# More added matrix products behind steps 2 and 3, a free bank for others, a third buffer for q and k

## The chip, the cores and the metric

The kernel runs on one core of one Trainium2 chip. The metric is the device time of one execution in microseconds (us). A core has engines that work side by side, each through its own queue of instructions in a fixed order: TensorE (PE in the profile, with its weight loads as PEld), VectorE (DVE), ScalarE (ACT), GpSimd (POOL) and SyncE (SP), which here only issues DMA transfers. An instruction waits in its queue until what it needs is done, and what is queued behind it waits too.

## What is computed

Windowed attention with linear biases over 8 batches, 8 heads, 576 positions and a head size of 64, and behind it a layer that takes the largest of three matrix products:

```python
scores = scale * np.matmul(q, k.transpose(0, 1, 3, 2))
mask = (rel >= 0) & (rel < window)                  # window = 128
scores = np.where(mask, scores + bias[None], -1000000000.0)
scores = scores - np.max(scores, axis=-1, keepdims=True)
attn = np.exp(scores)
attn = attn / (np.sum(attn, axis=-1, keepdims=True) + 1e-09)
attn_out = np.matmul(attn, v)
...
x = attn_out.transpose(0, 2, 1, 3).reshape(B * S, H * D)     # 4608 x 512
h = np.maximum(np.maximum(x @ w1, x @ w2), x @ w3)           # 4608 x 768
return h @ w_out                                             # 4608 x 512
```

## The kernel before

**Attention.** Work goes by *tasks*: one task is one pair of heads of one batch, so there are 4 tasks in a batch and 32 in all. A task has four blocks of 128 queries and a rest of 64; the rests of two tasks are done together. That gives 18 *steps* in a batch (`steps`, L406). The first batch runs: steps 0 to 4 belong to the first pair (step 4 holds the rests of the first and second pair), steps 5 to 8 to the second, steps 9 to 13 to the third, and so on.

For each two steps `products` (L413) puts score products of 64x64 tiles of PE into PSUM: into the tile `ps_s`, or, for steps 2, 6, 10 and 14 with the step behind each, into two banks of `ps_m`. For each step `score` (L438) has DVE move masked parts (L447, L450) and add the bias with a running minimum (L461); `exps` (L469) has ACT take exponentials; `sums_of` (L477) has ACT and DVE make the reciprocals; `normalise` (L482) multiplies, some on POOL (L487), some on ACT (L492); `turn` (L494) has PE transpose two steps into the bank `pt` (four instructions, L500), ACT copy them out (L504, L509, L512), and POOL cut out the window (L520, L524); `mix` (L529) multiplies with v (L545).

**The layer behind.** The weights come as packed integers. `fetch` (L150) loads a group (12 in all), `exponents` (L163) and `convert` (L173) turn it into floats on DVE, `part` (L210) splits it into a high and a low part and stores it; two buffers take the groups in turn, so a fetch waits until the group two before it is stored. `plain` (L769) runs the products of the first two batches (L791, L767 for three that begin early), `unit` (L812) those of the later ones in a form with fewer products (L846).

**Order.** All of it is written as events with due times, counted in steps (`at`, L872), sorted and called in that order (L950). The scheduler of the framework then lines up each engine's queue from its own estimate of what is ready, earlier calls first; `keep_in_program_order` puts an instruction behind the one called before it on its engine. From due time 46 on (`fix`, L935) this holds for nearly all of PE. A tile pool with n buffers hands a buffer on when the last reader of the tile in it is done.

**What the change touches.** `spin` (L372) issues n matrix products of zeros (128x512, bfloat16; L375) into the bank `pt`, the one in which `turn` puts its transposes. Their result is not read: the text calls them added products. Four run at the very start (L940), four are due at each of 3.45, 5.45, 7.45, ... 17.45 (L932), and ten stand behind the first plain products (L775). Each is kept behind what was called before it on PE. The group due at 3.45 comes behind the score products of steps 2 and 3, the one at 5.45 behind the transposes of steps 0 and 1 and the score products of steps 4 and 5.

`load` (L389) gets q and k of one task into a buffer of `qk_p` (two buffers), issued by SP (L394); `load_v` (L396) gets v. The start (L940 to L949) issues on SP the first pair, the first weight group, the second pair, v of the first pair, and the second weight group. q and k of the third pair are due at 0.6 (the second step of the first pair, L880) and take the buffer of the first pair, so they wait for the score products of step 4; v of the second pair is due at 2.6 and stands behind them in SP's queue.

The tiles `xs` (pool `xs_p`, seven buffers of the same size as a tile of `qk_p`) hold the attention's results of a batch, high and low part, for the layer behind. The first are written at due time 14.3 (L904).

Of the kernel before, what the change touches and what calls it, by code (L numbers as in the profile page):

```python
# [8 lines left out]
F32 = mybir.dt.float32  # L9
# [10 lines left out]
LOAD_I = 1  # L20
# [5 lines left out]
AT = 0, 3, 1, 2, 4, 6, 5  # L26
PLAIN_AT = (0, 6), (4, 5)
RING = 2
SPIN, FIRST_SPIN = 4, 4


FEW = 6
# [5 lines left out]
def attention_maxout_kernel(  # L38
# [12 lines left out]
    P = 128  # L51
    B, NP, _, _, S = qk.shape
# [5 lines left out]
    NB = S // P  # L58
# [3 lines left out]
    qk_p = ctx.enter_context(tc.tile_pool(name="qk_p", bufs=2))  # L62
# [4 lines left out]
    xs_p = ctx.enter_context(tc.tile_pool(name="xs_p", bufs=7))  # L67
# [5 lines left out]
    ps_m = ctx.enter_context(tc.tile_pool(name="ps_m", bufs=1, space=PSUM))  # L73
    ps_s = ctx.enter_context(tc.tile_pool(name="ps_s", bufs=1, space=PSUM))
    ps_t = ctx.enter_context(tc.tile_pool(name="ps_t", bufs=1, space=PSUM))
# [74 lines left out]
    def fetch(g):  # L150
        r = raws[g] = raw_tile()
        nc.sync.dma_start(r[:, SMALL:].bitcast(U8)[:, :16 * DM - 3], w_all[g].bitcast(U8)[:, 3:])
# [216 lines left out]
    idle = hs_p.tile([P, P + 512], mybir.dt.bfloat16, name="hs")  # L369
    nc.vector.memset(idle, 0.0)  # L370

    def spin(n):  # L372
        spun = ps_t.tile([P, 512], F32, name="pt")
        for _ in range(n):
            tc.keep_in_program_order(nc.tensor.matmul(  # L375
                spun, lhsT=idle[:, :P], rhs=idle[:, P:], start=True, stop=True, skip_group_check=True,
            ))
# [8 lines left out]
    tasks = [(b, hp) for b in range(B) for hp in range(NP)]  # L386
    qkt, vt = {}, {}


    def load(t):  # L390
        b, hp = tasks[t]
        qkt[t] = qk_p.tile([P, 2, S], F32, name="qk")
        for cs in (slice(0, 2 * P), slice(2 * P, S)) if t == 0 else (slice(0, S),):
            nc.sync.dma_start(qkt[t][:, :, cs], qk[b, hp, :, :, cs])  # L394

    def load_v(t):  # L396
        b, hp = tasks[t]
        vt[t] = v_p.tile([P, NB + 1, P], F32, name="v")
        nc.sync.dma_start(vt[t], v[b, hp])
# [10 lines left out]
    n_steps = len(steps) // B  # L410
# [199 lines left out]
    xs, hs, hq = {}, {}, {}  # L610
# [158 lines left out]
    def plain(b, v):  # L769
# [4 lines left out]
        if b == 0 and v == 1:  # L774
            spin(10)  # L775
# [96 lines left out]
    def at(when, what, *args):  # L872
        events.append((when, len(events), what, args))
# [2 lines left out]
    where = {x: s for s, x in enumerate(steps)}  # L876
    for s, (t, i) in enumerate(steps):
        c = s + shift[tasks[t][0]]
        if i == LOAD_I and t + 2 < len(tasks):
            at(c - 0.4, load, t + 2)  # L880
        if i == NB - 1 and t + 1 < len(tasks):
            at(c - 0.4, load_v, t + 1)
        if i == 0 and 0 < t < NP:
            at(c - 1, slopes, t)
            if t % 2 == 0:
                at(c - 1, slopes_t, t // 2)
        at(c + 0.04, score, s)
        at(c + 0.3, exps, s)
        if s % 2 == 0:
            at(c + 0.002, products, s)  # L890
            at(c + DRAIN[0].get(n_steps - s, LAG_T) + 0.003, turn, s)
        else:
            at(c + (0.6 if s == n_steps - 1 else 1.1), sums_of, s)
            at(c + (0.8 if s == n_steps - 1 else 1.5), normalise, s)
# [34 lines left out]
    at(2.06, weights, 1)  # L929
    for s in range(5, n_steps + 2):  # L930
        at(s + 0.2, weights, 1.4 if s > 5 else 0.6)
    for s in range(3, n_steps, 2):  # L932
        at(s + 0.45, spin, SPIN)

    def fix():  # L935
        nonlocal fixed
# [1 line left out]

    at(2 * n_steps + LAG_X + shift[2], fix)
    spin(FIRST_SPIN)  # L940
    load(0)
    nc.scalar.dma_start(dist[:, 2], c_ident)
    fetch(0)
    slopes(0)
    slopes_t(0)
    load(1)
    load_v(0)
    nc.scalar.copy(out=plus, in_=dist[:, 2])
    fetch(1)  # L949
    for _, _, what, args in sorted(events, key=lambda e: e[:2]):  # L950
# [39 lines left out]
```

## Time and profile before

| | us |
|---|---|
| median of 3 runs | 750.51 |
| lowest and highest of them | 749.09 and 750.65 |
| the profiled execution | 752.57 |
| its span, first to last instruction | 750.9 |

The profile is of one execution. Its page gives busy time by engine; its views give stretches of time with the busy time of each engine and the clock that was granted to PE (1.00 is 2.4 GHz, 0.50 is 1.2 GHz), the instructions in order of time, the waits, the DMA issues with the time until they landed, and the chain of waits that ended last. A row of the timeline merges neighbouring instructions of one kind: "x4" is four of them, and the time is that from the start of the first to the end of the last.

### The profile page before, as it was taken

How to read it: one execution, taken by the hardware profiler on the slowest of the kernel's cores; microseconds unless marked ns; L12 is line 12 of the kernel's file. 1: busy time of each engine (PE TensorE's matmuls, PEld its weight loads, DVE VectorE, ACT ScalarE, POOL GpSimd, SP SyncE). 2: the span in 40 equal slices, each digit the busy share in tenths (PEclk: the TensorE clock that was granted, in tenths of full speed). 3: DMA queues.
4: the chain of work that ended last, by engine and by line, in shares of the span. 5: the costliest groups of instructions: out<-in, count | busy, mean ns of one | idle time of the engine just before them, and what ended most of it. 6: DMA issues, size and time to landing. Idle time of an engine off the chain costs nothing.

```text
span 750.9 us, 19281 instructions
## 1 busy us (share of the span) xinstructions
PE 733.9 (98%) x7209; PEld 674.6 (90%) x7214; DVE 515.2 (69%) x1614; ACT 487.2 (65%) x1603; POOL 236.4 (31%) x451
## 2 busy tenths in 40 slices
PE   7999989999999999999999999999999999999998
PEld 3459988999999999999999999999999999999998
DVE  4888887536659477784778567794777747683673
ACT  5786976766667767676677757776666767552342
POOL 4661224645556123212222123222222122343100
PEclk8999999999999999999999999999999999999999
DMA  7877999759998489855988378864988468899611
GB/s 252 274 282 298 330 340 331 253 187 340 361 349 275 134 279 303 273 181 192 322 294 276 116 266 304 291 213 146 330 289 273 163 228 272 252 291 355 230 61 64
DMA packets 57085, 192.81 MB, mean 257 GB/s; under 512 B 5792, under 2 KB 24480, under 8 KB 50464
## 3 DMA queue, kind: packets, MB, share of 16 engines
q0 software_dynamic: 20304, 108.54, 43.9%
q1 hardware_dynamic: 36400, 82.85, 31.2%
q8 instruction: 57, 0.93, 0.5%
q14 instruction: 36, 0.29, 0.1%
q10 hardware_dynamic: 288, 0.20, 0.1%
HBM read 156.95 MB, written 34.60 MB: 255 GB/s over the span
## 4 chain that ended last, share of the span: by engine, by line
PE 77%; DVE 11%; ACT 7%; DMA 2%; issue 1%; POOL 1%; SPq 0%; DVEq 0%; ACTq 0%; POOLq 0%
PE ps_m L846 46%; PE ps_m L791 16%; PE ps_s L431 5%; PE pt L500 4%; PE ps_x L567 4%; DVE hs L615 2%; DVE hq L733 2%; ACT p L473 2%; DVE t L732 2%; DMA qk<-in_qk 1%; PE ps_x L545 1%; DMA hs<-in_w_all 1%; ACT p L492 1%; DVE t L618 1%; DVE xs L615 1%
## 5 line engine op out<-in xcount | busy, mean ns | idle before, releaser
L846 PE MATMUL ps_m<-xs,ring 128*128 128x288 f32 x2160 | 302.7, 297 | 0.6
L846 PEld LDWEIGHTS ps_m<-xs,ring 128*128 128x128 f32 x2160 | 290.1, 188 | 3.7 <-ACT t L863 3.4
L520 POOL TENSOR_SCALAR_AFFINE_SELECT pp<-pr 128x256 f32<-128x256 f32 x112 | 53.9, 482 | 277.2 <-ACT pr L504 154.0
L473 ACT ACTIVATE p<-s,st 128x128 f32<-128x128 f32 x288 | 114.7, 400 | 20.8 <-DVE st L461 17.2
L863 ACT COPY t<-ps_m 128x288 f32<-128x288 f32 x196 | 76.7, 394 | 71.2 <-PE ps_m L846 69.5
L791 PE MATMUL ps_m<-xs,ring 128*128 128x288 f32 x846 | 118.1, 297 | 2.8 <-DVE hq L808 2.2
L791 PEld LDWEIGHTS ps_m<-xs,ring 128*128 128x128 f32 x846 | 113.3, 188 | 4.1 <-DVE hq L808 2.4
L367 POOL DMA_DIRECT2D ring<-keep x103 | 55.5, 539 | 165.5 <-PE ps_m L846 157.3
L846 PE MATMUL ps_m<-hs,ow 128*128 128x288 f32 x756 | 105.8, 297 | 0.4
L846 PEld LDWEIGHTS ps_m<-hs,ow 128*128 128x128 f32 x756 | 100.9, 188 | 2.6 <-ACT t L863 1.2
L492 ACT ACTIVATE p<-p,st 128x128 f32<-128x128 f32 x252 | 84.6, 393 | 24.1 <-DVE st L480 24.1
L732 DVE TENSOR_TENSOR t<-ps_m,t 128x288 f32<-128x288 f32 x108 | 48.8, 453 | 42.8 <-PE ps_m L846 32.5
L461 DVE CUSTOM_DVE_ANT_0 s<-ps_s,bias 128x128 f32<-128x128 f32 x240 | 60.6, 285 | 9.0 <-POOL bias_t L112 3.4
L431 PE MATMUL ps_s<-qk 64*64 64x192 f32 (+1 forms) x1088 | 62.0, 319 | 3.4 <-DMA qk<-in_qk 2.4
L614 ACT CAST hs<-hq 128x288 fp32r<-128x288 f32 x96 | 40.2, 432 | 30.8 <-DVE hq L733 18.1
L473 ACT ACTIVATION_READ_ACCUMULATOR p<-s,st 128x1 f32 x288 | 55.3, 192 | 0.0
L567 PE MATMUL ps_x<-pp,v 64*64 64x64 f32 (+3 forms) x1456 | 53.4, 274 | 0.1
L567 PEld LDWEIGHTS ps_x<-pp,v 64*64 64x64 f32 x1456 | 41.7, 133 | 10.5 <-issue 8.6
L500 PE MATMUL pt<-plus,p 128*128 128x128 f32 x288 | 48.5, 289 | 2.0 <-POOL p L487 1.3
L524 POOL TENSOR_SCALAR_AFFINE_SELECT pp<-pr 128x256 f32<-128x256 f32 (+1 forms) x112 | 50.0, 447 | 1.1
L733 DVE TENSOR_TENSOR hq<-t,hq 128x288 f32<-128x288 f32 x108 | 48.8, 457 | 2.1
L601 DVE TENSOR_TENSOR xk<-ps_x,xk 128x256 f32<-128x256 f32 (+3 forms) x56 | 25.4, 454 | 36.0 <-ACT xk L600 36.0
(94 smaller groups left out, 942.0 us busy)
## 6 DMA issues: line engine op xcount, KB each, us to landing
ring<-keep POOLq DMA_DIRECT2D x51, 1024.0 KB, 7.4
ring<-keep POOLq DMA_DIRECT2D x61, 768.0 KB, 6.1
qk<-in_qk SPq DMA_DIRECT2D x31, 576.0 KB, 5.3
hs<-in_w_all SPq DMA_DIRECT2D x12, 1023.6 KB, 7.2
v<-in_v SPq DMA_DIRECT2D x32, 320.0 KB, 6.5
outT<-t SPq DMA_DIRECT2D x64, 144.0 KB, 1.8
keep<-ring SPq DMA_DIRECT2D x9, 768.0 KB, 6.5
plain<-hs SPq DMA_DIRECT2D x12, 512.0 KB, 4.0
```

The lines of the kernel that those rows point to most:

```text
L367: nc.gpsimd.dma_start(wts[n, a], keep[n % 9][a])
L431: pe(nc.tensor.matmul(ps[j][d:d + D, o:o + k1 - k0], lhsT=qkt[u][j * D:(j + 1) * D, 0, q0:q0 + D], rhs=qkt[u][j * D:(j + 1) * D, 1, k0:k1] ...
L461: first(nc.vector.tensor_tensor_reduce(out=x, in0=ps[j][:, P:2 * P], in1=below, scale=-0.125, scalar=3.0e38, op0=ALU.add, op1=ALU.min, acc ...
L473: nc.scalar.activation(p[:, j], x, AF.Exp, bias=st[:, 0, a, j:j + 1], scale=-1.0, accum_out=st[:, 1, a, j:j + 1])
L492: nc.scalar.activation(p[:, j], p[:, j], AF.Copy, scale=st[:, 2, a, j:j + 1])
L500: pe(nc.tensor.transpose(out=pt[:, a, j], in_=p[:, j], identity=ident))
L567: pe(nc.tensor.matmul(x[j * D:(j + 1) * D, r, o:o + rhs.shape[1]], lhsT=vv[k, i, j * D:(j + 1) * D], rhs=rhs[k], start=start, stop=True, s ...
L732: nc.vector.tensor_tensor(out=s, in0=ps, in1=e, op=ALU.add)
L733: nc.vector.tensor_tensor(out=h, in0=s, in1=h, op=ALU.max)
L791: pe(nc.tensor.matmul(ps, lhsT=lt, rhs=rt, start=n == 0 and not (b == 0 and v < EARLY), stop=n == len(pairs) - 1, skip_group_check=True,))
L846: pe(nc.tensor.matmul(part_of[n, {2: 0, 5: 0, 6: 0, 3: 1}.get(kk, kk)], lhsT=lt, rhs=rt, start=first, stop=i == len(pairs) - 1, skip_group ...
L863: nc.scalar.copy(out=e, in_=ps)
```

## The change

1. The group of added products due at 3.45 has 13 instead of 4 (`WAIT_SPIN`) and writes the bank `ps_m2`, which at that time nothing else uses. The group due at 5.45 is dropped. The groups due at 7.45, 9.45, 11.45, 13.45 and 15.45 keep their four and write `ps_m2` too; the one at 17.45 stays as it was.
2. q and k of the third pair (task 2) go into a buffer of `xs_p`. They are issued at the start, behind v of the first pair, and v of the second pair behind them, both ahead of the second weight group. Their events at 0.6 and 2.6 fall away. The fourth pair then takes the first pair's buffer of `qk_p`, the fifth the second's; from the sixth pair on each waits for the same pair as before.

```diff
-SPIN, FIRST_SPIN = 4, 4
+SPIN, FIRST_SPIN, WAIT_SPIN = 4, 4, 13
...
-    def spin(n):
-        spun = ps_t.tile([P, 512], F32, name="pt")
+    def spin(n, spare=False):
+        spun = (ps_m if spare else ps_t).tile([P, 512], F32, name="ps_m2" if spare else "pt")
...
-        qkt[t] = qk_p.tile([P, 2, S], F32, name="qk")
+        qkt[t] = (xs_p if t == 2 else qk_p).tile([P, 2, S], F32, name="xs" if t == 2 else "qk")
...
-        if i == LOAD_I and t + 2 < len(tasks):
+        if i == LOAD_I and 2 < t + 2 < len(tasks):
             at(c - 0.4, load, t + 2)
-        if i == NB - 1 and t + 1 < len(tasks):
+        if i == NB - 1 and 1 < t + 1 < len(tasks):
             at(c - 0.4, load_v, t + 1)
...
-    for s in range(3, n_steps, 2):
-        at(s + 0.45, spin, SPIN)
+    at(3.45, spin, WAIT_SPIN, True)
+    for s in range(7, n_steps, 2):
+        at(s + 0.45, spin, SPIN, s < n_steps - 2)
...
     load_v(0)
+    load(2)
+    load_v(1)
     nc.scalar.copy(out=plus, in_=dist[:, 2])
     fetch(1)
```

## Rows read from the trace of the kernel before

**Rows 1.** The page: busy us (share of the span), instructions of each engine.

```profile
PE 733.9 (98%) x7209; PEld 674.6 (90%) x7214; DVE 515.2 (69%) x1614; ACT 487.2 (65%) x1603; POOL 236.4 (31%) x451
```

**Rows 2.** Stretches: length, busy of PE, PEld, DVE, ACT, POOL; clock, DMA, GB/s.

```profile
8.85:11.26 2.41, 0.00 (x1) 0.00 (x1) 1.47 (x7) 0.79 (x4) 1.56 (x4) 0.86 1.05 427
11.26:17.30 6.04, 5.82 (x34) 2.71 (x35) 3.10 (x16) 3.93 (x18) 1.50 (x4) 0.50 0.66 249
...
25.00:54.20 29.20, 27.68 (x229) 14.88 (x227) 25.00 (x84) 24.37 (x89) 18.06 (x27) 1.00 0.86 310
...
57.52:123.00 65.48, 61.58 (x645) 56.78 (x645) 55.42 (x160) 51.33 (x145) 17.35 (x31) 1.00 0.89 326
123.00:750.90 627.90, 623.44 (x6204) 593.62 (x6203) 418.22 (x1307) 394.87 (x1308) 186.28 (x362) 1.00 0.74 248
```

**Rows 3.** Timeline of PE: start, us, line, operation, count, idle before.

```profile
7.35 1.04 PE L375 MATMUL pt<-hs 128*128 128x512 bf16 x4
8.31 0.54 PE L431 MATMUL ps_s<-qk 64*64 64x192 f32 x2
11.26 1.34 PE L431 MATMUL ps_s<-qk 64*64 64x192 f32 x14 [2.41 <-DMA qk<-in_qk]
12.53 1.11 PE L500 MATMUL pt<-plus,p 128*128 128x128 f32 x4
13.57 1.97 PE L431 MATMUL ps_m<-qk 64*64 64x256 f32 x12
15.48 0.61 PE L375 MATMUL pt<-hs 128*128 128x512 bf16 x1
...
17.30 0.69 PE L431 MATMUL ps_m<-qk 64*64 64x256 f32 x4
17.91 0.44 PE L500 MATMUL pt<-plus,p 128*128 128x128 f32 x2
...
19.80 0.77 PE L431 MATMUL ps_s<-qk 64*64 64x192 f32 x14
```

**Rows 4.** Timeline of SP's DMA issues: start, us of issuing.

```profile
2.82 0.43 SPq L394 DMA_DIRECT2D qk<-in_qk  x1
...
3.77 0.74 SPq L152 DMA_DIRECT2D hs<-in_w_all  x1
...
20.42 0.33 SPq L394 DMA_DIRECT2D qk<-in_qk  x1
```

**Rows 5.** DMA issues at 2.82 and 3.77 us: KB, us to landing.

```profile
qk<-in_qk SPq DMA_DIRECT2D x1, 576.0 KB, 8.4
...
hs<-in_w_all SPq DMA_DIRECT2D x1, 1023.6 KB, 10.7
```

**Rows 6.** Timeline of PE, later rows.

```profile
28.33 0.66 PE L500 MATMUL pt<-plus,p 128*128 128x128 f32 x4
...
39.05 1.02 PE L375 MATMUL pt<-hs 128*128 128x512 bf16 x4 [0.55 <-ACT pr L504]
```

**Rows 7.** Groups by form: added products, 7.3-8.4 and 15.4-17.3 us; busy, mean ns.

```profile
L375 PE MATMUL pt<-hs 128*128 128x512 bf16 x4 | 1.0, 382 | 0.0
...
L375 PE MATMUL pt<-hs 128*128 128x512 bf16 x3 | 1.7, 626 | 0.2 <-issue 0.2
```

**Rows 8.** Timeline of DVE and ACT, 12 to 23 us.

```profile
12.66 0.43 DVE L450 COPY_PREDICATED ps_s<-prev,ps_s 128x256 f32<-128x256 uint8 x1 [1.14 <-PE ps_s L431]
...
15.31 0.68 ACT L492 ACTIVATE p<-p,st 128x128 f32<-128x128 f32 x2
...
18.04 0.30 DVE L447 COPY_PREDICATED ps_m<-prev,ps_m 128x128 f32<-128x128 uint8 x1 [2.15 <-PE ps_m L431]
...
19.34 0.59 ACT L504 COPY pr<-pt 128x512 f32<-128x512 f32 x1 [2.58 <-PE pt L500]
...
22.92 0.77 DVE L166 TENSOR_SCALAR hs<-hs 128x1024 int8<-128x1024 int8 x1
```

**Rows 9.** Chain of waits that ended last, in order of time, from 57.5 us.

```profile
70.65 7.38 DMA hs<-in_w_all
```

## The prediction

> **What bounds the kernel now.** I read the page's engine shares first [rows 1]: TensorE (PE) is busy 98% of the span, so a change can only pay where PE stands, runs slowly, or runs matrix products that compute nothing. The table of stretches says where that is [rows 2]: from 123 us to the end PE stands about 4.5 us in 628, so that part can only be moved as a whole. From 57.5 to 123 us it stands 3.9 us. From 25 to 54 us it is busy 27.7 of 29.2 us, but every engine is busy there too. Only the first 20 us show something large: PE does nothing from 8.85 to 11.26 us, and in the 6 us behind that its granted clock is 0.50, the lower of its two levels (1.2 GHz instead of 2.4).
>
> The timeline of PE shows what happens in there [rows 3]. Four added products run from 7.35 us, behind the score products of steps 2 and 3. Then two products of step 4 run and the other 14 wait until 11.26 us. These need q and k of the second pair: that load was issued at 2.82 us and landed 8.4 us later, at 11.2 [rows 4, 5]. PE stood 2.4 us, and its clock fell before it went on. Until 17.3 us it works off, at the lower clock, 14 products, the four transposes of steps 0 and 1, 12 products of steps 6 and 7, the four added products due at step 5 (15.48 to 17.30 us) and the last 4 products. The same operations elsewhere show the price of the clock: 14 products take 1.34 us here and 0.77 at 19.80 us; four transposes 1.11 us here and 0.66 at 28.33 [rows 3, 6]; an added product takes 626 ns here and 382 at 7.35 us [rows 7].
>
> Then I read who waited for PE [rows 8]. VectorE (DVE) stood 2.15 us until 18.04, for the last 4 products. ScalarE (ACT) stood 2.58 us until 19.34, for the transposes of steps 2 and 3. So the delay of PE reaches all engines, and the chain of waits goes on through that ACT copy.
>
> **The fill behind steps 2 and 3.** Thirteen added products take the place of four. Four take 1.04 us, one 0.38, so one more costs 0.22 [rows 3, 7]; thirteen run from 7.35 to 7.35 + 12 x 0.22 + 0.38 = 10.4 us. The two early products of step 4 (0.54 us) end at 10.9, and the other 14 start at 11.26 as before. The nine extra ones cost nothing: the load hides them, and by 0.4 us they do not outlast it. What stays idle is 0.4 us instead of 2.4. I take it that the clock then stays at its higher level, since PE stands 0.55 us at 39.05 [rows 6] in a stretch whose granted clock is 1.00 [rows 2].
>
> With the higher clock the 14 products end at 12.0 (0.57 earlier), the transposes at 12.7, and the 16 products of steps 6 and 7, about 2.5 us at the lower clock, take some 1.5 in the ratio of the transposes: 14.2 us. Before they ended at 18.0.
>
> **No added products at step 5.** This removes 1.8 us of PE between two products that DVE waits for, and is contained in the 14.2.
>
> **What is late next.** The 3.8 us that PE gains there are not all kept. The transposes of steps 2 and 3 need normalised probabilities, which ACT finished at 15.99 us (15.31 + 0.68) [rows 8]. That date hangs on DVE, which waited until 12.66 us for step 4's products, then ran a weight conversion, four score operations and the reciprocal. All of these move only by the 0.57 us of the 14 products, so the probabilities are there at 15.4. In the run before, the first transpose (17.91) to the ACT copy (19.34) took 1.43 us, with two products of attention and v between them. The first half does not need ACT's part, which saves a little: I put the ACT copy at 16.6. That is 2.7 us earlier, with 2.5 (the whole 1.43 behind 15.4) and 3.6 (only PE's own dates) as ends. DVE's 2.15 us and ACT's 2.58 us of standing are what these engines move into, so all of them run some 2.7 us early from there.
>
> **The free bank.** The groups due at steps 7, 9, 11, 13 and 15 write a bank that nobody reads, instead of the transposes' bank, which ACT must empty first. In the trace that emptying held PE once, 0.55 us at 39.05 [rows 6]. Their number stays, so their own time stays. They may now come ahead of other work in PE's queue: between 0.55 us gained and the rival below. I take 0, because PE is nearly full there and the order within a full queue moves no sum.
>
> **The third pair's own buffer.** Its q and k, and the second pair's v, are now issued at about 4 us, before the second weight load. On the DMA-issuing engine (SP) the load of the fourth pair comes next: it waits for the first pair's buffer, free at 12.0 with the products above, and goes out then instead of at 20.42 [rows 4]. Nothing of PE waited for any of these pairs, so this gains nothing by itself; it takes 576 KB away from behind 20.42. What is queued behind the moved issues is the second weight load: it landed at 3.77 + 10.7 = 14.5 us [rows 4, 5]. With 896 KB more ahead at the 427 GB/s of that stretch [rows 2] it lands 2.1 us later, at 16.6. DVE takes it up at 22.92 [rows 8], at 20.2 after the change, so 3.6 us of cover are left. If that cover were gone, DVE would wait for the excess. The load that PE waits for at 11.26 is ahead of the moved ones. Its delay lies between 0 and 2.1 us (all 896 KB served before it). I take 0: it landed before the larger weight load that was issued less than 1 us after it, by 3.3 us [rows 4, 5].
>
> The Trainium skill, "DMA: Bandwidth & Descriptors", Queues, rings and completion order, says that each DMA engine takes the descriptors of a ring in ring order, but that completion is not first in, first out. By the first half the sum is -2.7; by the second, read at its worst, it would be the -0.6 of the late load below. The order of landings agrees with the first half.
>
> **Sum.** Span 750.9 us, and 752.57 for the profiled execution, which leaves 1.7 us around it. -2.7 gives a span of 748.2 and 749.9 for such an execution. The profiled one lies 2.1 above the median of the runs (750.51), so against the median the time is 747.8.
>
> Of the 3.8 us that PE gains, the granted clock carries 2.0. The Trainium skill, "TensorE: Matmul & The Clock Gate", Seeing it yourself, warns that the records of the clock have been unreliable. If they were wrong here, only step 5's group would be gained, some 1.8 us on PE. The durations of three kinds of operation, all 1.6 to 1.7 times as long, bear the record out.
>
> **Rivals.**
> 1. *The gain is swallowed later.* Between 57.5 and 123 us PE stands 3.9 us [rows 2], and the chain of waits runs there through the weights: a weight load of 7.38 us from 70.65 [rows 9], then ACT and DVE. If these keep their dates, PE merely waits longer: 0.3 us left, 750.2. For it: DMA is busy 0.89 there. Against it: the weights' conversions stand in the same DVE and ACT queues as the scores, whose dates move, and the transfers wait for these.
> 2. *The load comes late.* With the 2.1 us bound the 14 products start at 13.4; the idle time is back and the clock may fall. Of 2.7 us about 0.6 is left: 749.9. Against it: the order of landings.
> 3. *Slower: the added products come ahead of work that is waited for.* In a bank that is always free the five groups can be put straight behind the transposes, ahead of the score products and the products with v. Each holds PE 0.96 us (4 x 0.22 + 0.08 of loading). If each lies wholly on the chain: 5 x 0.96 - 2.7 = +2.1, 752.6. It decides where what follows a group on PE is ready at once and the others wait for it. For it: PE is 95% busy there. Against it: behind transposes the chain goes through ACT and GpSimd before PE is needed again, and PE's total stays.
> 4. *More.* The weights move by more than PE, since 576 KB leave their way and SP waits less, and up to half of the 3.9 us goes too: about 745.5.
>
> **How the numbers follow.** Forecast 0.60; swallowed 0.14; late load 0.08; slower 0.10; more 0.08. A difference under 0.2% (1.5 us) cannot be told from none here. Faster: 0.60 + 0.08 = 0.68; within: 0.14 + 0.08 = 0.22; slower: 0.10. The forecast alone spans 746.9 to 748.0 by its ends of 3.6 and 2.5, and some 0.5 more at either end for the 0.55 us that the free bank can give or take. For 8 in 10 the range takes in both middle rivals and cuts most of the slower one and of the fourth: 745.8 to 750.6.
>
> **What would show it.** Right: PE busy from 7.35 to nearly 11 us; granted clock 1.00 through 10 to 18 us; products of steps 6 and 7 done near 14.2; the ACT copy now at 19.34 near 16.6; the first plain product, now at 57.52, near 54.8; the weight load near 16.6 without a wait for it on DVE. Wrong: the 14 products later than 11.5 us; a clock of 0.50 anywhere before 20 us; a shift at 57.5 that is gone at 123; groups of added products with DVE or ACT standing for the products behind them.

## The result and the profile after

The changed kernel takes 758.19 us (median of 4 runs, 754.17 to 758.97), the kernel before 749.97 (4 runs): a ratio of 1.0102, interval 1.0068 to 1.0136. The forecast was 747.8 us, in a range of 745.8 to 750.6. The sign was wrong, and the time lies outside the range. The profiled execution took 758.93 us, with a span of 757.2.

The page's engine shares answer [rows 1]:

```profile
PE 737.5 (97%) x7214; PEld 678.5 (90%) x7219; DVE 515.2 (68%) x1614; ACT 487.6 (64%) x1603; POOL 238.1 (31%) x451
```

The busy time of VectorE (DVE) is the same to a tenth, and ScalarE (ACT) has 0.4 us more. TensorE (PE) is busy 3.6 us longer and stands 19.7 us instead of 17.0. Apart from PE's five more added products no engine got more work to do; PE's other operations run longer, at a mean granted clock of 0.988 instead of 0.995.

The stretches of [rows 2] and the one between them; columns: length, busy of PE, PEld, DVE, ACT, POOL, granted clock, DMA share, GB/s:

```profile
8.85:11.26 2.41, 1.26 (x6) 0.37 (x4) 0.68 (x2) 0.27 (x2) 1.07 (x3) 1.00 1.02 414
11.26:17.30 6.04, 5.27 (x43) 2.72 (x43) 4.94 (x27) 4.45 (x19) 1.97 (x4) 0.72 0.92 369
25.00:54.20 29.20, 25.08 (x195) 14.95 (x196) 20.33 (x69) 19.95 (x73) 14.24 (x21) 0.86 0.73 270
54.20:57.52 3.32, 1.92 (x10) 0.86 (x10) 3.25 (x13) 2.88 (x11) 0.77 (x2) 1.00 0.61 146
57.52:123.00 65.48, 61.79 (x618) 54.80 (x618) 54.31 (x150) 50.19 (x139) 20.92 (x30) 0.97 0.85 311
```

The first two rows are better than before: PE works where it stood, and the clock of the six microseconds behind is 0.72 instead of 0.50. The third row is where the time goes. From 25 to 54 us DVE is busy 20.3 us instead of 25.0, ACT 19.9 instead of 24.4, PE 25.1 instead of 27.7, and the clock is 0.86 instead of 1.00. Every engine does less in the same time there.

PE's timeline, as in [rows 3] and further on:

```profile
5.54 1.19 PE L431 MATMUL ps_m<-qk 64*64 64x256 f32 x16
6.67 2.98 PE L375 MATMUL ps_m<-hs 128*128 128x512 bf16 x13
9.58 0.54 PE L431 MATMUL ps_s<-qk 64*64 64x192 f32 x2
12.03 0.81 PE L431 MATMUL ps_s<-qk 64*64 64x192 f32 x14 [1.91 <-DMA qk<-in_qk]
12.77 1.11 PE L500 MATMUL pt<-plus,p 128*128 128x128 f32 x4
...
22.23 0.44 PE L500 MATMUL pt<-plus,p 128*128 128x128 f32 x2 [1.04 <-POOL p L487]
23.25 0.69 PE L500 MATMUL pt<-plus,p 128*128 128x128 f32 x2 [0.58 <-POOL p L487]
23.73 1.91 PE L375 MATMUL ps_m<-hs 128*128 128x512 bf16 x4
25.58 1.19 PE L545 MATMUL ps_x<-pp,v 128*64 128x256 f32 x6
...
42.37 0.65 PE L545 MATMUL ps_x<-pp,v 128*64 128x256 f32 x4 [1.63 <-POOL pp L520]
45.83 4.58 PE L767 MATMUL ps_m<-xs,ring 128*128 128x288 f32 x18
...
64.89 1.32 PE L791 MATMUL ps_m<-xs,ring 128*128 128x288 f32 x8
```

The thirteen products end at 9.65 us, not at 10.4, since the score products ahead of them ended earlier. The load lands later than in the profile before, so PE still stands 1.91 us. The transposes behind it already run at the lower level (1.11 us). Behind two short waits at 22 us (1.04 and 0.58) the clock is lower again, with four added products, those due at 9.45, in front of products with v. The first plain product of L791 starts at 64.89 us instead of 57.52 (forecast: 54.8), so 7.4 us are lost by there; the span is 6.3 longer.

SyncE's issues, as in [rows 4]:

```profile
3.77 0.71 SPq L394 DMA_DIRECT2D xs<-in_qk  x1
4.52 1.22 SPq L399 DMA_DIRECT2D v<-in_v  x1
5.78 0.67 SPq L152 DMA_DIRECT2D hs<-in_w_all  x1
```

Their landings, as in [rows 5]: the load issued at 2.82 us, which PE waits for, and the weight load issued at 5.78; columns: KB, us to landing:

```profile
qk<-in_qk SPq DMA_DIRECT2D x1, 576.0 KB, 9.2
...
hs<-in_w_all SPq DMA_DIRECT2D x1, 1023.6 KB, 11.7
```

The first took 9.2 us to land, not 8.4. The two moved loads behind it need not be the reason: over the profiled executions of the 14 kernels whose loads stand as before, the same load takes from 8.4 (kernel before, count_alone) to 9.7 us (drop_seven), and over the five with the moved loads from 8.3 to 9.5. In bank_alone, one of the 14, PE waits for it until 12.48 us:

```profile
12.48 1.29 PE L431 MATMUL ps_s<-qk 64*64 64x192 f32 x14 [4.44 <-DMA qk<-in_qk]
```

So the landing at 11.2 us, from which the forecast was worked out, was an early one. The weights are there at 17.5 us (forecast: 16.6); DVE takes them up at 21.96, so their cover held.

ACT's timeline, as in [rows 8]:

```profile
18.38 0.59 ACT L504 COPY pr<-pt 128x512 f32<-128x512 f32 x1 [1.40 <-PE pt L500]
...
24.35 0.36 ACT L509 COPY pp<-pt 128x256 f32<-128x256 f32 x1
27.92 0.64 ACT L552 COPY xk<-ps_x 128x576 f32<-128x576 f32 x1 [3.20 <-PE ps_x L545]
28.45 0.40 ACT L473 ACTIVATE p<-s,st 128x128 f32<-128x128 f32 x1
```

The copy forecast for 16.6 us comes at 18.38, one microsecond earlier than before. At 24.35 us the order itself is new. In the kernel before, four exponentials (L473) and two normalising steps (L492) follow that copy, and L552 comes behind them, without a wait:

```profile
27.58 0.64 ACT L552 COPY xk<-ps_x 128x576 f32<-128x576 f32 x1
```

Here L552 stands ahead of them and waits 3.20 us, and the exponentials wait behind it. Nobody edited that: the scheduler puts every engine's instructions in an order by its own estimate of when things are ready, and the change moved the estimate. Comparing the two programs, the lists of DVE (1616 instructions) and ACT (1319) differ in 252 and 221 places.

### The profile page after: what moved, and what is told of

The parts are those of the page before. It is cut to its first block, busy times and chain, and to the rows that moved or that the text cites. A ratio compares the mean times of both kernels' runs of the same rounds, so it can differ in the third digit from the quotient of the medians.

```text
span 757.2 us, 19291 instructions
## 1 busy us (share of the span) xinstructions
PE 737.5 (97%) x7214; PEld 678.5 (90%) x7219; DVE 515.2 (68%) x1614; ACT 487.6 (64%) x1603; POOL 238.1 (31%) x451
## 4 chain that ended last, share of the span: by engine, by line
PE 77%; DVE 9%; ACT 3%; issue 1%; POOL 1%; DVEq 0%; POOLq 0%; ACTq 0%
PE ps_m L846 45%; PE ps_m L791 18%; PE ps_s L431 5%; PE ps_x L567 5%; PE pt L500 4%; DVE hs L615 2%; DVE hq L733 2%; DVE t L732 2%; ACT p L473 1%; DVE t L618 1%; ACT p L492 1%; DVE xk L601 1%; ACT t L863 0%; ACT hs L614 0%; DVE xs L615 0%
## 5 line engine op out<-in xcount | busy, mean ns | idle before, releaser
L473 ACT ACTIVATE p<-s,st 128x128 f32<-128x128 f32 x288 | 114.7, 401 | 19.9 <-DVE st L461 17.7
L791 PE MATMUL ps_m<-xs,ring 128*128 128x288 f32 x846 | 118.4, 299 | 0.0
L791 PEld LDWEIGHTS ps_m<-xs,ring 128*128 128x128 f32 x846 | 114.6, 190 | 0.6 <-DVE xs L615 0.3
L492 ACT ACTIVATE p<-p,st 128x128 f32<-128x128 f32 x252 | 84.6, 393 | 25.3 <-DVE st L480 25.3
L431 PE MATMUL ps_s<-qk 64*64 64x192 f32 (+1 forms) x1068 | 59.4, 317 | 3.9 <-DVE st L461 2.0
L473 ACT ACTIVATION_READ_ACCUMULATOR p<-s,st 128x1 f32 x288 | 55.3, 192 | 0.0
L524 POOL TENSOR_SCALAR_AFFINE_SELECT pp<-pr 128x256 f32<-128x256 f32 (+1 forms) x112 | 54.1, 483 | 1.1
L500 PE MATMUL pt<-plus,p 128*128 128x128 f32 x288 | 50.2, 294 | 3.0 <-POOL p L487 2.0
L500 PEld LDWEIGHTS pt<-plus,p 128*128 128x128 f32 x288 | 31.1, 143 | 24.2 <-issue 12.7
```

What stands on the lines that cost most here:

```text
L431: pe(nc.tensor.matmul(ps[j][d:d + D, o:o + k1 - k0], lhsT=qkt[u][j * D:(j + 1) * D, 0, q0:q0 + D], rhs=qkt[u][j * D:(j + 1) * D, 1, k0:k1] ...
L473: nc.scalar.activation(p[:, j], x, AF.Exp, bias=st[:, 0, a, j:j + 1], scale=-1.0, accum_out=st[:, 1, a, j:j + 1])
L492: nc.scalar.activation(p[:, j], p[:, j], AF.Copy, scale=st[:, 2, a, j:j + 1])
L500: pe(nc.tensor.transpose(out=pt[:, a, j], in_=p[:, j], identity=ident))
L791: pe(nc.tensor.matmul(ps, lhsT=lt, rhs=rt, start=n == 0 and not (b == 0 and v < EARLY), stop=n == len(pairs) - 1, skip_group_check=True,))
```

## The experiments

Theory at the start: the parts add up, and the two that were taken as nothing cost. In the table, "order" is how many places of DVE's and ACT's instruction lists differ from the kernel before (one moved instruction can count more than once). Each run reports the mean granted clock of its span. Over 135 runs of the kernel before, compared within each round of runs, the time falls by 0.54 us for each thousandth of it, so the difference of the means is split into what that slope makes of the clock and a rest. The split is an estimate: it does not say why the clock differs. The interval of the rest is twice its standard error.

| run | ratio, interval | order | clock, against before | us by clock | rest, us |
|---|---|---|---|---|---|
| loads_alone | 1.0081, 1.0042 to 1.0119 | 275, 193 | 0.9918, 0.9953 | 1.9 | 5.0 ± 1.2 |
| loads_again | 1.0002, 0.9979 to 1.0025 | 0, 0 | 0.9953, 0.9964 | 0.6 | 0.2 ± 0.6 |
| count_alone | 0.9965, 0.9946 to 0.9984 | 16, 18 | 0.9991, 0.9953 | -2.1 | -0.1 ± 0.8 |
| fill13_keep5 | 0.9988, 0.9963 to 1.0012 | 0, 0 | 0.9980, 0.9964 | -0.9 | 0.4 ± 0.8 |
| none5 | 1.0024, 0.9998 to 1.0050 | 16, 18 | 0.9956, 0.9964 | 0.4 | 1.4 ± 1.1 |
| bank_alone | 1.0050, 1.0026 to 1.0073 | 240, 176 | 0.9943, 0.9953 | 0.5 | 3.5 ± 0.8 |
| spins_all | 1.0025, 1.0004 to 1.0047 | 110, 78 | 0.9946, 0.9953 | 0.4 | 2.4 ± 0.9 |
| bank_later | 1.0050, 1.0024 to 1.0075 | 99, 62 | 0.9964, 0.9964 | 0.0 | 4.4 ± 0.7 |
| bank_quiet | 0.9994, 0.9971 to 1.0017 | 0, 0 | 0.9961, 0.9954 | -0.4 | 0.2 ± 0.7 |
| bank_nine | 0.9999, 0.9980 to 1.0017 | 9, 4 | 0.9947, 0.9954 | 0.4 | 0.1 ± 0.8 |
| bank_seven | 1.0052, 1.0033 to 1.0071 | 231, 172 | 0.9930, 0.9954 | 1.3 | 2.8 ± 0.7 |
| seven_late | 1.0029, 1.0004 to 1.0054 | 0, 0 | 0.9953, 0.9954 | 0.1 | 1.7 ± 0.8 |
| drop_seven | 1.0035, 1.0011 to 1.0060 | 0, 0 | 0.9934, 0.9965 | 1.7 | 1.3 ± 1.0 |
| bank_thirteen | 1.0030, 1.0000 to 1.0059 | 93, 69 | 0.9945, 0.9954 | 0.5 | 1.9 ± 1.4 |
| drop_thirteen | 1.0030, 1.0012 to 1.0048 | 90, 61 | 0.9968, 0.9965 | -0.2 | 2.3 ± 1.2 |
| all_held | 0.9980, 0.9960 to 0.9999 | 0, 0 | 0.9973, 0.9954 | -1.0 | -0.2 ± 0.7 |
| held_none5 | 0.9987, 0.9965 to 1.0008 | 16, 18 | 0.9976, 0.9954 | -1.2 | -0.2 ± 0.8 |

**The parts.** Each of the three parts alone, and the two that concern the added products together. loads_alone has only the third pair's load and buffer:

```diff
-        qkt[t] = qk_p.tile([P, 2, S], F32, name="qk")
+        qkt[t] = (xs_p if t == 2 else qk_p).tile([P, 2, S], F32, name="xs" if t == 2 else "qk")
...
+    load(2)
+    load_v(1)
```

> Only the second part of the change: q and k of the third pair in a buffer of xs_p, issued at the start with v of the second pair; the added products as before. Theory (the loss comes from the added products' free bank: groups that come ahead of the products with v, for which ScalarE and then VectorE wait): between -1 and +1 us against the kernel before. Rival 1 (the moved loads do it: the second pair's q and k land 0.8 us later, and SP's and the engines' queues come out in another order): +4 to +8 us. Rival 2 (the thirteen products and the clock): 0.

count_alone has 13 products at 3.45 and none at 5.45, all in the transposes' bank:

```diff
-    for s in range(3, n_steps, 2):
+    at(3.45, spin, 13)
+    for s in range(7, n_steps, 2):
```

> Thirteen added products instead of four behind steps 2 and 3, none at step 5, all still in the transposes' bank; loads as before. The order of the queues is nearly that of the kernel before. Theory: the fill itself is sound, -1 to -3 us, with the first plain product 1 to 3 us earlier. Rival 1 (loads): the same. Rival 2 (the fill does not hold the clock and delays products): 0 to +3 us, with the granted clock at 0.50 around 11 to 18 us as before.

bank_alone keeps the counts and puts six groups (3.45, 7.45 and on to 15.45) into the free bank; spins_all has both:

```diff
-        at(s + 0.45, spin, SPIN)
+        at(s + 0.45, spin, SPIN, s < n_steps - 2 and s != 5)
```

> The counts as before (four at each of the eight places), but the groups due at 3.45, 7.45, 9.45, 11.45, 13.45 and 15.45 write the free bank; 5.45 and 17.45 stay in the transposes' bank; loads as before. Theory: +3 to +7 us, ScalarE standing at line 552 and 504 for products behind a group. Rivals 1 and 2: between -1 and +1 us.

> The whole first part (thirteen, none at step 5, free bank for the groups to 15.45), loads as before. Theory: +2 to +6 us, the free bank's loss less what the thirteen bring. Rival 1: -3 to 0 us. Rival 2: 0 to +3 us.

Measured, by the ratios: loads +6.1 us (five runs, with a wide interval), counts -2.6, bank +3.8, products' parts together +1.9. Within their intervals the parts multiply: 1.0081 x 0.9965 x 1.0050 = 1.0096 against 1.0102 for the whole. So the counts give about the 2.7 us that were expected of them, and both parts taken as nothing cost more than that. In count_alone PE does what the forecast says of it; its timeline:

```profile
7.77 3.39 PE L375 MATMUL pt<-hs 128*128 128x512 bf16 x13
11.09 0.94 PE L431 MATMUL ps_s<-qk 64*64 64x192 f32 x16
11.95 0.66 PE L500 MATMUL pt<-plus,p 128*128 128x128 f32 x4
```

And its stretch behind the old gap, columns as above:

```profile
11.26:17.30 6.04, 5.39 (x52) 2.68 (x51) 4.90 (x24) 4.38 (x19) 1.62 (x4) 1.00 0.73 266
```

In the timeline of loads_alone (its profiled execution is the slowest of its five) DVE shows what the load's early buffer did to the order around 44 us (the first four lines), and what followed:

```profile
43.59 0.68 DVE L166 TENSOR_SCALAR hs<-hs 128x1024 int8<-128x1024 int8 x1
44.20 0.28 DVE L461 CUSTOM_DVE_ANT_0 s<-ps_s,bias 128x128 f32<-128x128 f32 x1
44.41 1.22 DVE L177 CUSTOM_DVE_ANT_0 hs<-hs 128x1024 int32<-128x1024 int8 x1
45.54 0.28 DVE L461 CUSTOM_DVE_ANT_0 s<-ps_s,bias 128x128 f32<-128x128 f32 x1
...
53.33 0.29 DVE L461 CUSTOM_DVE_ANT_0 s<-ps_s,bias 128x128 f32<-128x128 f32 x1 [3.79 <-PE ps_s L431]
```

In the kernel before, four score operations come first there and the conversion behind them:

```profile
43.94 0.29 DVE L461 CUSTOM_DVE_ANT_0 s<-ps_s,bias 128x128 f32<-128x128 f32 x1
44.15 0.28 DVE L461 CUSTOM_DVE_ANT_0 s<-ps_s,bias 128x128 f32<-128x128 f32 x1
...
44.95 0.29 DVE L461 CUSTOM_DVE_ANT_0 s<-ps_s,bias 128x128 f32<-128x128 f32 x1
45.16 0.28 DVE L461 CUSTOM_DVE_ANT_0 s<-ps_s,bias 128x128 f32<-128x128 f32 x1
45.37 0.69 DVE L166 TENSOR_SCALAR hs<-hs 128x1024 int8<-128x1024 int8 x1
```

Both kernels reach this point at the same time (the masked scores ahead of it start at 43.26 and 43.38 us). With the conversion lined up between them the scores come later, and DVE stands 3.79 us at 53.33.

**Is it the load or the order?** loads_again is loads_alone with a second, useless load of the same size at the place in SyncE's queue that the third pair's load left, so that the weights stand behind as many loads as before:

```diff
+    def again():
+        tc.keep_in_program_order(nc.sync.dma_start(xs_p.tile([P, 2, S], F32, name="xs"), qk[0, 3]))
...
+    at(9.6, again)
```

> As loads_alone, and q and k of the fourth pair of the first batch are loaded a second time, into a buffer that nobody reads, at the place in SP's queue where a load stood before the change. With that the queues of PE, VectorE, ScalarE and GpSimd come out instruction for instruction as in the kernel before; what stays of the change is the early issue, the own buffer, and 576 KB more to move. Theory (loads_alone lost its 6 us through the order in which the scheduler lined up the queues, the weights' conversions ahead of the scores): -1 to +1.5 us against the kernel before. Rival (the load that PE waits for lands later, or the transfers collide): +4 to +8 us.

The whole loss is gone, though the load of the second pair is as late as in loads_alone (9.3 and 9.5 us to landing). Its PE timeline has a longer wait than before and the lower clock behind it (its lines are three further down, L434 is L431):

```profile
12.20 1.34 PE L434 MATMUL ps_s<-qk 64*64 64x192 f32 x14 [3.02 <-DMA qk<-in_qk]
```

So of the loads part neither the late landing nor the buffer cost anything that shows. What cost goes back with the place in SyncE's queue: the order of every engine, and with it the times of the weight loads behind it (the one at 43.14 us in loads_alone goes out at 45.48 here and 45.56 before). The two are not held apart; that DVE stands for PE's products at 53.33, and not for a transfer, speaks for the order. (The run also has 576 KB more to move.)

**The counts taken apart.** fill13_keep5 has 13 products at 3.45 and leaves the four at 5.45 there; none5 has four and none:

```diff
-        at(s + 0.45, spin, SPIN)
+        at(s + 0.45, spin, 13 if s == 3 else SPIN)
```

> Only thirteen instead of four added products behind steps 2 and 3, in the transposes' bank; the group of step 5 stays. All other queues are instruction for instruction as before. Theory (the fill holds the clock and this is its price alone): -0.5 to -2 us. Rival (all of count_alone's gain is the group of step 5): 0.

> Four added products behind steps 2 and 3 as before, none at step 5. Theory: -0.5 to -2 us, since the clock is low there and the group holds PE 1.8 us ahead of products that VectorE waits for. Rival (all of count_alone's gain is the clock): 0.

Neither can be told from no change, and singly they do not give the sum: -0.9 and +1.8 us against -2.6 together. By the split the gain of the pair is all clock: 7 of 10 runs of count_alone have a mean granted clock of 1.00, and 11 of the 135 runs of the kernel before. At that clock the pair shows no gain: the median of the 7 is 750.0 us, that of the 11 is 748.8.

**The free bank.** First theory: groups that no longer wait for ACT run ahead of the score products. bank_later holds four of them half a step back, behind these products:

```diff
+        x = s in (3, 7, 9, 11, 13)
+        at(s + (1.0025 if x and s > 3 else 0.45), spin, SPIN, x)
```

> Counts as before; the group due at 3.45 and those of steps 7, 9, 11 and 13 write the free bank, but the latter four are due half a step later, pinned behind the score products of the next two steps; the groups of steps 5, 15 and 17 stay as before. Theory (bank_alone lost 4 us because groups stood ahead of products that others wait for): -1 to +1.5 us. Rival (the free bank itself costs, or the group due at 3.45 that starts earlier): +3 to +5 us.

It is as slow as bank_alone, so the theory falls in this form. Next, single groups, in the free bank at their old due times (`s in (3, 11, 15)`, `s == 7`, `s == 9`, `s == 13` in place of the condition above):

> Counts as in the kernel before; three of the six groups that the change puts into the free bank go there (due 3.45, 11.45 and 15.45), the others stay. With these three the order of the instructions on VectorE, ScalarE, GpSimd and SyncE stays what it was; TensorE's alone differs, in the places of the added products. Theory A (the bank part costs its 3.8 us because the scheduler lines up the other engines' work anew): no difference, within 1.5 us of the kernel before. Theory B (the groups themselves cost it, as they start ahead of work that is waited for; 3.8 us over six groups are 0.6 each): 1.9 us slower.

> Counts as before; only the group due at 7.45 goes into the free bank. VectorE's order differs in about 230 of 1616 places, ScalarE's in about 170 of 1319, as in the run with all six. Theory A (the new order costs it): 2 to 4 us slower, with most of the 3.8 us in this one group. Theory B (each group costs alike): 0.6 us slower, which three rounds hardly tell from none.

> Counts as before; only the group due at 9.45 goes into the free bank. ScalarE's queue differs in one thing: the copy of the first pair's mixed rows (L552) stands ahead of six activations of the softmax instead of behind them; VectorE's in nine places around it. Theory A1 (that copy, which waits for the products of the mix with the exponentials queued behind it, is what costs the bank part): 2 to 4 us slower. Theory A2 (it is the longer new order further on that costs it): within 1.5 us of the kernel before. Theory B: 0.6 us slower.

> Counts as before; only the group due at 13.45 goes into the free bank: the last of the six to be tried. VectorE's order differs in about 93 places, ScalarE's in 69, in a later stretch than with the group of 7.45. If that of 7.45 holds the bank part's whole loss (the six parts add up to 3.8 us): within 1 us of the kernel before. If every new order costs something: 1 to 4 us slower.

Four of the six groups cost nothing that shows, three of them with the others' order as before. bank_nine has the copy L552 ahead of the exponentials, as the changed kernel has, and ACT waits 1.98 us for it; the time doesn't show it. So the kind of wait that caught the eye in the profile after (there 3.20 us) need not cost anything. The groups of 7.45 and 13.45 cost 3.9 and 2.3 us; they add up to more than the 3.8 of all.

Do these two cost by the others' order, or by their place in PE's own? seven_late has the first one due at 8.05, which leaves the others' order as it was; drop_seven and drop_thirteen leave one group out altogether, with no free bank:

```diff
-        at(s + 0.45, spin, SPIN)
+        at(s + (1.05 if s == 7 else 0.45), spin, SPIN, s == 7)
...
-        at(s + 0.45, spin, SPIN)
+        if s != 7:
+            at(s + 0.45, spin, SPIN)
```

> As the run with the group of 7.45 alone in the free bank (5.2 thousandths slower), but that group is due at 8.05, behind the score products. Same group, same bank, same four products; the order of VectorE, ScalarE, GpSimd and SyncE is then that of the kernel before, and only TensorE's differs, in 23 places. Theory A (the new order of the other engines cost it): within 1.5 us of the kernel before. Theory B' (the free bank at step 7, or the products as such, cost it): 3 to 4 us slower, as with the group at 7.45.

> The kernel before without the group of four at 13.45: 1.0 us less work of TensorE, no free bank anywhere. The order of VectorE's and ScalarE's work is then that of the run with this group in the free bank, but for 5 and 6 places (against 90 and 61 places from the kernel before). Theory A (the new order cost that run its 2.3 us): slower all the same, 1 to 3 us. Theory B (the group's place in TensorE's own queue cost it): not slower, 0 to 1 us faster.

> The kernel before without the group of four at 7.45; the order of VectorE, ScalarE, GpSimd and SyncE is that of the kernel before, TensorE's differs by the missing group and the places around it. The run with this group later in the free bank was 2.2 us slower with the same order of the others. Theory B (there the products stood ahead of the mix, and that cost it): without them no slower, 0 to 1 us faster. Theory C (it cost the filling of the gap that the group left; the clock falls more often): 1 to 3 us slower here too.

drop_thirteen has less to do and no free bank, and with bank_thirteen's order (but for 5 and 6 places) it has its loss: 1.0030 both. So the loss goes with the order. A rival is left: the group may have been worth something in its old place. The mean clock of drop_thirteen, 0.9968 against 0.9965, does not speak for it, but no run moves this group with the order held.

The group of 7.45 is another case. With the free bank but a later due time, 2.2 us of its 3.9 stay (seven_late). Without it the kernel is 2.6 us slower with every other engine's order as before. The kernel before, with that group in its place, at 20.50 us:

```profile
20.50 1.04 PE L375 MATMUL pt<-hs 128*128 128x512 bf16 x4
...
23.19 0.44 PE L500 MATMUL pt<-plus,p 128*128 128x128 f32 x2 [0.71 <-POOL p L487]
24.21 0.44 PE L500 MATMUL pt<-plus,p 128*128 128x128 f32 x2 [0.58 <-POOL p L487]
```

drop_seven, PE at the same transposes:

```profile
24.54 0.44 PE L500 MATMUL pt<-plus,p 128*128 128x128 f32 x2 [1.19 <-POOL p L487]
25.56 0.64 PE L500 MATMUL pt<-plus,p 128*128 128x128 f32 x2 [0.58 <-POOL p L487]
26.13 1.54 PE L545 MATMUL ps_x<-pp,v 128*64 128x256 f32 x6
```

And a stretch of drop_seven behind them, columns as above:

```profile
25.00:30.00 5.00, 4.40 (x21) 2.17 (x23) 2.25 (x11) 2.87 (x13) 2.92 (x4) 0.66 1.02 377
```

That group filled part of a gap in front of the transposes. Without it PE stands 1.19 us instead of 0.71, and the clock behind is 0.66 in this execution where it was 1.00. One execution proves little: held_none5 stands 1.61 and 0.58 us at these transposes and its clock stays 1.00. Over all runs drop_seven has a mean clock of 0.9934 against 0.9965: by the split 1.7 us, beside a rest of 1.3. seven_late has the added products behind the gap (at 25.45 us, in 1.92 us, at the lower clock), in front of work that others wait for; its mean clock over all runs is that of the kernel before, and its loss lies in the rest.

Neither is what the free bank does to this group at its old due time. In bank_seven it runs ahead of the products with v, and the wait at the transposes is as before:

```profile
21.09 0.44 PE L500 MATMUL pt<-plus,p 128*128 128x128 f32 x2 [0.71 <-POOL p L487]
...
84.86 0.40 PE L791 MATMUL ps_m<-xs,ring 128*128 128x288 f32 x1 [1.17 <-ACT ring L200]
...
116.23 1.34 PE L431 MATMUL ps_s<-qk 64*64 64x192 f32 x16 [2.11 <-DVE st L461]
```

In this execution (the fastest of nine) the clock is 1.00 to 57 us, and the first plain product of L791 comes at 54.55 us, 3 us ahead of the kernel before. The span is 2.1 us longer all the same, so the loss lies behind that point: PE waits there for weights from ACT (1.17 us) and for a score operation of DVE (2.11 us, where the kernel before waits 0.95), with a clock of 0.95 in both stretches from 57.52 to 90 and from 90 to 123 us. These are the engines whose order is new, so the order is the likely cause of this group's 3.9 us too; no run has that order without the group's new place.

**All parts with the order held.** all_held has the 13 products, the early load with loads_again's second one, and the free bank for the groups of 3.45, 11.45 and 15.45, and keeps the group of 5.45. held_none5 leaves that group out, with the free bank at 3.45 alone. On top of loads_again:

```diff
-    for s in range(3, n_steps, 2):
-        at(s + 0.45, spin, SPIN)
+    at(3.45, spin, 13, True)
+    for s in range(5, n_steps, 2):        # held_none5: from 7
+        at(s + 0.45, spin, SPIN, s in (11, 15))        # held_none5: without the condition
```

> All three parts of the change, as far as the order of VectorE, ScalarE and GpSimd stays that of the kernel before: 13 products at due 3.45 in the free bank, those of 11.45 and 15.45 there too, 4 at 5.45 kept (without them the order changes), the third pair's load early into its own buffer, and a second, useless load of the same 576 KB where the third pair's load stood before. Theory A (order costs what the change lost, parts by themselves cost nothing): as the 13 products with 4 kept, 0.9 us faster, between 0 and 2.5. Theory B (the bank's groups and the early load cost by themselves): 2 to 4 us slower.

> The change with the free bank for the group at 3.45 alone and the place of the third pair's load in SyncE's queue taken by a useless second load of the same size: 13 products there, none at 5.45, groups of four from 7.45 on in the old bank, the third pair's load early into its own buffer. The other engines' order is that of the run with the counts alone (16 of VectorE's 1616 places differ from the kernel before, 18 of ScalarE's). Theory A: as the counts alone, 2.6 us faster (1 to 4). Theory B (bank or early load cost by themselves): none faster, up to 4 us slower.

Both are on the side of faster: 0.9980 and 0.9987 (the second interval takes in no change). Nothing of the loads' loss is left, with the early load and the free bank at 3.45 in both. The bank's two costly groups, those of 7.45 and 13.45, are in neither, so these runs say nothing about them. The gain of the counts is there in part (1.5 and 1.0 us of 2.6); their intervals overlap, so whether the rest is lost isn't settled. The best kernel measured is count_alone, 0.9965.

## Why the prediction was wrong

*The fill and step 5* (sum -2.7): measured -2.6, but not by the path given, so that the sizes agree is in part luck. The steps hold in count_alone: the products fill the wait, the clock is 1.00 through 11.26 to 17.30 us, and the transposes are at 11.95. The first plain product of L791 comes at 53.97 us, where 54.8 was forecast. But step 5 wasn't worth a share of its own, and the gain lies in how often whole runs keep the upper clock (rest -0.1 us). The low clock behind the first wait, 2.0 of the 3.8 us, was read from one execution: bank_seven stands 2.84 us in the same wait and its clock stays 1.00.

*The free bank*, taken as 0: measured +3.8. The failing sentence is that the order within a full queue moves no sum. What it leaves out is that the bank is a resource in the scheduler's estimate: when it is free, other engines' work is lined up anew. The two groups that cost alone, 13.45 (2.3 us) and 7.45 (3.9 us), are the two with a new order in many places; of the others three leave the order as it was and one changes it in 9 and 4 places. For these two the order is argued and not isolated.

*The third pair's own buffer*, taken as 0: measured +6.1. That nothing of PE waited for these pairs was right, as loads_again shows. The load that PE waits for landed 0.8 us later than in the profile before, but it does so with unmoved loads too, and in loads_again it cost nothing. What failed is the unspoken step that the queues keep their order. SyncE's later issues move up, presumably the weights are ready earlier in the scheduler's estimate, and DVE's conversions are put among the scores. The page of the Trainium skill cited in the prediction ("DMA: Bandwidth & Descriptors", Queues, rings and completion order) says that completion is not first in, first out. Here the loads of q, k and v landed in the order of issue: in the changed kernel those issued at 2.82, 3.29, 3.77 and 4.52 us at 12.0, 12.8, 14.2 and 15.0.

*Rivals.* The late load (749.9): the load was late, but loads_again has it as late and loses nothing. The slower one (752.6) had the right bank and the right sign. Its picture, products in front of work that is waited for, is to be seen at 23.73 us; but those are the group of 9.45, which costs nothing in bank_nine, and four of the six groups cost nothing. Its price fell short of the 758.2, and no rival let the third pair's buffer cost more than a late load. That the gain is swallowed later (750.2) happened in part: in count_alone 3.6 us at the first plain product of L791 are 2.4 at the end (span 748.5). The fourth has a slip: half of 3.9 us off 747.8 is 745.9, not 745.5. No case at all had the other engines' order in it, and that is where the range failed.

*What would show it.* Three of the signs of being wrong came. The 14 products start at 12.03 us, later than 11.5, though they do so in bank_alone too. The clock is 0.50 before 20 us: the transposes at 12.77 us run at the lower level. And ACT stands 3.20 us for products behind the added ones at 23.73, which run at the lower level too.

What stays open: whether the order is all of the loss of the groups of 7.45 and 13.45; and why four products at 5.45 are worth keeping with four at 3.45 (none5 is not faster) but not with 13. none5's profiled execution stands 1.61 us at the transposes at 23.04 and has a clock of 0.73 from 25 to 30 us; but held_none5 stands 1.61 us there too and keeps 1.00, so this alone is no answer.

## What to carry to other kernels

Where a scheduler lines up the engines' queues, a buffer that comes free earlier is no free gift: before costing it at nothing, compare the order of every engine's instructions, and to test the part by itself, hold that order (a dummy transfer in the old place did it here). Filler work is worth what its place is worth: ask of each group which gap it fills, and what the clock does when it is no longer there. A wait that looks large in the new profile (ACT's 3.20 us here) proves nothing until a run has it alone. And a date read from one profile, such as the landing of a load or the fall of the clock, may be that execution's own: look at it in the profiles of other kernels with the same start.

## What the runs showed of the hardware

Behind the wait for the same load PE's granted clock fell in one execution and not in another. Up to the wait for the second pair the kernel before, bank_nine and bank_seven have the same instructions on PE; PE waits 2.41, 3.39 and 2.84 us, and from 11.26 to 17.30 us the clock is 0.50, 0.72 and 1.00. The same holds for short waits close together: with 1.19 and 0.58 us drop_seven has a clock of 0.66 from 25 to 30 us, with 1.05 and 0.58 spins_all has 1.00, and with 1.61 and 0.58 none5 has 0.73 and held_none5 1.00.

The mean granted clock of whole runs of one program differs: for the kernel before from 0.99 (six runs, on average 754 us) to 1.00 (eleven, 749 us). Part of what an edit is worth lies in how often a run falls on which side.

One load of 576 KB, issued at 2.8 us behind the same transfers, took 8.4 to 9.7 us to land over 14 kernels that do not differ in their loads.
